# Order of loads, casts and second-layer splits around the first expert tile of an attention-plus-MoE kernel

## Chip, cores and metric

The kernel runs on one core of one Trainium2 chip. The metric is the device time of one execution in microseconds (us). A core has five engines with instruction streams of their own: PE (TensorE, matrix products), DVE (VectorE), ACT (ScalarE), POOL (GpSimd) and SP (SyncE, which here only issues transfers). Each works through its stream in order and waits on semaphores for the others. PEld is PE loading weights. Transfers issued by SP and by POOL stand in two queues, called q1 (SP) and q0 (POOL) in the profile, which are served by the same 16 DMA engines.

## The reference

Softmax attention with capped scores, then a top-1 mixture of experts (MoE) with a modality bias on the gate. Sizes: 8 batches of 448 tokens, 12 heads of 64; 3584 tokens of width 768, 8 experts, inner width 1024; all in float32.

```python
scores = cap * np.tanh(scale * np.matmul(q, k.transpose(0, 1, 3, 2)) / cap)
attn = np.exp(scores - np.max(scores, axis=-1, keepdims=True))
attn = attn / (np.sum(attn, axis=-1, keepdims=True) + 1e-09)
attn_out = np.matmul(attn, v)                      # -> x: [3584, 768]
...
logits = x @ w_gate + modality_bias[modality_id]
e_idx = np.argmax(logits, axis=1)                  # one expert per token
gate_w = probs[np.arange(N), e_idx]
for e in range(E):
    mask = e_idx == e
    h = np.maximum(x[mask] @ w1[e], 0.0)
    out[mask] = gate_w[mask, None] * (h @ w2[e])
```

## The kernel before

**Attention** (the first 332 us) runs over 24 units d, each two head pairs of one batch (three units to a batch), in 7 steps s of 64 keys. PE makes scores (`sc`), ACT applies tanh and exp (`pt`), PE multiplies by the values (`xT`), DVE sums the weights (`tot`). Finished tokens are written to a table `xd` in DRAM. `route` picks each token's expert and scatters the token's number and gate weight into a map `mapd` in DRAM, grouped by expert, with four indirect transfers on POOL for each batch.

**The MoE part** works on slots: 384 tokens of one expert, in three row tiles t of 128. `rows` loads the slot's part of the map (`mt`, 3 KB), `gather` fetches the tokens with three indirect transfers on POOL (`xg`), PE transposes them (`move`), ACT and DVE write them as a high and a low half (`take`, tile `x`). The weights are split the same way: `split_w` has ACT cast a raw chunk to its high half (`ah` for the first layer, `bh` for the second) and DVE subtract that from the raw chunk for the low half (`al`, `bl`). The first layer's weights `w1` have 6 chunks of 512 KB (index k), the second layer's `w2` 8 chunks of 384 KB (index f). Raw chunks go through a ring of four buffers (`raw`); a load waits until the chunk that held its buffer has been split. `ffn1` makes `h` (tile `ph` to `hh`, `hl`), `ffn2` makes the output rows (`py`; ACT scales them into `ot`, and an indirect transfer on POOL writes them out). Every product is three matmuls: high by high, high by low, low by high.

**The first slot overlaps the end of attention.** From the counts of the first seven batches `early_slot` picks an expert with a full slot. At unit 22, step 2, SP is given the load of `mt`, then POOL the three gathers; chunks 0 and 1 of `w1` are loaded by SP, chunks 2 to 5 by POOL (`load_w1` inside `attention`; the last two have buffers of their own, `spare`). The slot's `ffn1` carries hooks. Its first three column tiles are made together, chunk by chunk (per chunk k three tiles of three matmuls), and after single chunks, and after column tile f = 3, a piece of leftover attention work is put in: `last_sums`, `last_turn`, `last_route`, `last_rank`, then `slots`, the table of all other slots. In this slot `ffn2` is called with `wait=2`: for t = 0 both halves of the output are accumulated side by side in the two `py` banks (f outermost), and the transposes of the next slot's tokens come only after the first half of t = 1.

**What sets the order.** A scheduler places instructions by dependences and by the order of the code; what is given to `pin` (and all loads made by `load`) keeps the program's order on its engine. A register load may be tied behind an instruction (`register(..., after)`). The splits of the second layer's first four chunks come after `slots` (hook f = 3), the next four after `ffn1`, and `load_w1` of the next slot's expert before `ffn2`.

Of the kernel before, what the change touches and what calls it, by code (L numbers as in the profile page):

```python
# [49 lines left out]
B, H, S, D = 8, 12, 448, 64  # L50
C, CP = 4, 112
NP = H // 2
NT, DM, FF, E, NM = B * S, H * D, 1024, 8, 2
# [14 lines left out]
ENDS = ((2, 2, 1), (3, 2), (3, 2, 1))  # L68
MAXS = RB + E - 1
W2_EARLY = 4  # L70
LEAD = 3
CAP_FAST = 64.0
NU = NP // 2
# [6 lines left out]
class Program:  # L80
# [340 lines left out]
    def attention(self, firsts, rp, xp):  # L421
        tc, nc = self.tc, self.nc
        pe, pin, V = nc.tensor, self.pin, nc.vector
        with ExitStack() as st:
# [154 lines left out]
            for n in range(END):  # L579
                d, s = divmod(n, STEPS)  # L580
                if s == 0:
                    fetch(d + 1)
                    if d == 0:
                        self.fetch_bias()
                    if d == 2:
                        self.empty_map()
                scores(n)
                while n not in held and added <= n - BEHIND + (d == ND - 1):
                    add(added)
                    added += 1  # L590
                if (d, s) == (1, 3):
                    self.gate_bias()
                if (s == 6 or s == 1) and d != SOON + 2:
                    go_on()
                if s == 4 and d >= 2 and d != SOON + 2:
                    turn(d - 2)
                    go_on()
                    tokens(d - 2)
                    logits(d - 2)
                if (d, s) == (SOON + 3, 0):  # L600
                    sums(d - 2)
                if s == 5 and d and d != SOON + 2:
                    sums(d - 1)
                    if d >= 2 and d - 2 != SOON and (d - 2) % NU == NU - 1:
                        start_route((d - 2) // NU)
                for m in due[n]:
                    weigh(m)
                    if m % STEPS == STEPS - 1:
                        keep(m // STEPS)
                if (d, s) == (SOON + 1, 6):  # L610
                    turn(SOON)
                    logits(SOON)
                    start_route(SOON // NU, firm=True)
                    go_on()
                    go_on()
                if (d, s) == (SOON + 2, 1):
                    go_on()
                    meta = self.early_slot(self.cpool, self.ps_r)
                    self.first_e = self.expert(meta, 0)
                    load_w1((0, 1), self.first_e)  # L620
                if (d, s) == (SOON + 2, 2):
                    tokens(SOON, nc.sync, (self.ps_r, "small"), (ps_g, "glog"))
                    maps = self.rows(meta, 0, early=True)
                    self.gather(maps, known=NT - S)
                    load_w1((2, 3, 4, 5), self.register(nc.gpsimd, meta[0:1, 0:1], E - 1), nc.gpsimd)
                if (d, s) == (SOON + 2, 6):
                    split(0, V, V)
                if (d, s) == (SOON + 3, 5):
                    split(1, V, V)
# [30 lines left out]

            def last_sums():
                ready(3)
                sums(ND - 1, self.ps_y, "py")

            def last_turn():
                ready(5)
                turn(ND - 2)
                logits(ND - 2)

# [62 lines left out]
    def gather(self, mt, n=TW, known=NT):  # L732

        for t in range(n):
            got = self.nc.gpsimd.indirect_dma_start(
                self.xg.bitcast(F32)[:, t], None, self.xd[:known],
                bass.IndirectOffsetOnAxis(ap=mt.bitcast(I32)[:, t, 0:1], axis=0),
                bounds_check=known - 1, oob_is_err=False,
            )
            self.pin(got)  # L740

    def load_raw(self, e, src, k, width, dst=None, queue=None):
        raw = self.stg.tile([128, FF], F32, name="raw") if dst is None else dst
# [89 lines left out]
            finish(ph, f)  # L833
            hook("f", f)

    def ffn2(self, mt, n, between=(), wait=0):

        nc = self.nc
        between = list(between)
        for t in range(n):  # L840
# [19 lines left out]
            for half in range(2):  # L860
                if not both:
                    for f in range(FC):
                        products(half, f)
                cs = slice(half * HALF, (half + 1) * HALF)
                nc.scalar.mul(ot[:, cs], pys[half][:, :HALF], mt[:, t, 1:2])  # L865
                left = 2 * n - 1 - (2 * t + half)
                if 2 * t + half >= wait:
                    for _ in range(-(-len(between) // left) if left else 0):
                        between.pop(0)()
# [5 lines left out]
    def run_slot(self, cur, n, ahead=None, raws=(), hooks=None):  # L875
# [5 lines left out]
        moves = []  # L881
        if hooks:
            work = hooks[("f", 3)]
            hooks[("f", 3)] = lambda: (work(), self.load_w2(cur[0], raws, range(W2_EARLY)))
        elif n == TW:
            self.load_w2(cur[0], raws)
        nxt = ahead() if ahead and not hooks else None
# [3 lines left out]
            nxt = ahead()  # L891
        if n < TW:
            self.load_w2(cur[0], raws)
        if nxt:
            self.load_w1(nxt[0])
            moves = [lambda k=k: self.transpose(k, self.ps_t, "ptr", n=nxt[2]) for k in range(KC)]
        self.ffn2(cur[1], n, between=moves, wait=2 if raws else 0)
        return nxt

    def run_slots(self, cur, hooks):  # L900
# [240 lines left out]
```

## Time and profile before

| | us |
|---|---|
| times of three runs | 868.88, 873.9, 873.51 (median 873.51) |
| profiled execution, its own time | 873.96 |
| its span, first to last instruction | 872.4 |
| PE busy in the span | 842.1 (97%) |
| ACT busy | 533.0 (61%) |
| DVE busy | 514.4 (59%) |
| POOL busy | 134.5 (15%) |
| DMA, mean over the span | 157 GB/s |

Times inside the profile count from the span's start. A row of the timeline gives start, duration, engine, line of the kernel, operation and tiles, and in brackets how long the engine was idle just before and what ended that. Line 767 is the transpose of gathered tokens, 777 and 778 ACT's and DVE's part of `take`, 753 and 754 those of `split_w`, 799, 800 and 803 the first layer's products, 850 the second layer's, 865 the scaling of output rows, 735 the gather, 726 the load of `mt`, 275 the scatter into the map, 547 the write of tokens to `xd`, 92 a load.

### The profile page before, as it was taken

To read this page: it belongs to the slowest core of one execution; us is meant where nothing else is said; L and a number is where in the kernel's file an instruction comes from. 1 tells how busy PE (TensorE), PEld (TensorE's weight loads), DVE (VectorE), ACT (ScalarE), POOL (GpSimd) and SP (SyncE) were. 2 spreads that over 40 slices of the span, in tenths; PEclk is the share of its full clock that TensorE was granted. 3 is DMA by queue.
4 is the path that set the end of the run, shared out by engine and by line. 5 is a ranking of instruction groups with operands and counts; after the bars stand their busy time and mean duration, and the time that the engine had idled before them with its cause. 6 is when DMAs were issued, how large, how long until landed. Compare 5 with 4: busy or idle time off the path is not lost. (4 is left out here: it accounts for less than half of the span.)

```text
span 872.4 us, 15882 instructions
## 1 busy us (share of the span) xinstructions
PE 842.1 (97%) x6216; PEld 639.4 (73%) x6216; DVE 514.4 (59%) x896; ACT 533.0 (61%) x627; POOL 134.5 (15%) x155
## 2 busy tenths in 40 slices
PE   7999999999999998989999999999999999999996
PEld 2344434434444336979999999999999999989995
DVE  3679687788888796854433444334344433467851
ACT  6999989999999894354342444334344433446541
POOL 2002020202020232242030120202002030011000
PEclk9999999999999998989999999999999999999998
DMA  5354444554453674297355473535646353457640
GB/s 168 105 170 100 156 135 144 143 166 98 165 123 132 170 185 130 46 323 238 95 168 196 144 255 105 189 109 173 223 139 228 115 156 142 158 158 240 225 159 6
DMA packets 44284, 136.92 MB, mean 157 GB/s; under 512 B 8526, under 2 KB 9102, under 8 KB 44192
## 3 DMA queue, kind: packets, MB, share of 16 engines
q1 hardware_dynamic: 34432, 101.00, 36.5%
q0 software_dynamic: 9616, 34.74, 13.2%
q8 instruction: 52, 0.85, 0.4%
q14 instruction: 40, 0.33, 0.1%
q10 hardware_dynamic: 144, 0.00, 0.0%
HBM read 114.20 MB, written 22.69 MB: 157 GB/s over the span
## 5 line engine op out<-in xcount | busy, mean ns | idle before, releaser
L459 ACT ACTIVATE pt<-sc,isc 128x896 f32<-128x896 f32 x168 | 161.3, 995 | 17.2 <-PE sc L455 17.0
L803 PE MATMUL ph<-x,al 128*128 128x384 f32 (+2 forms) x528 | 167.9, 318 | 0.0
L850 PE MATMUL py<-bh,hh 128*128 128x384 f32 x464 | 160.2, 345 | 4.9 <-ACT ot L865 3.3
L850 PE MATMUL py<-bl,hh 128*128 128x384 f32 x464 | 157.1, 339 | 0.6 <-DVE bl L754 0.6
L850 PE MATMUL py<-bh,hl 128*128 128x384 f32 x464 | 157.1, 339 | 0.0
L462 ACT ACTIVATE pt<-pt,cabs 128x1792 f32<-128x1792 f32 x84 | 150.4, 1790 | 2.7
L485 PE MATMUL xT<-pt,va 64*64 64x448 f32 x1344 | 146.2, 538 | 0.3 <-DVE xT L492 0.3
L473 DVE TENSOR_TENSOR tot<-tot,pt 128x896 f32<-128x896 f32 x120 | 130.3, 1086 | 7.5 <-ACT pt L462 4.1
L800 PE MATMUL ph<-x,ah 128*128 128x384 f32 x384 | 129.2, 336 | 0.4 <-DVE x L778 0.4
L799 PE MATMUL ph<-x,ah 128*128 128x384 f32 x384 | 129.5, 337 | 0.0
L754 DVE TENSOR_TENSOR bl<-raw,bh 128x768 fp32r<-128x768 f32 x88 | 81.3, 955 | 50.5 <-ACT bh L753 44.0
L485 PEld LDWEIGHTS xT<-pt,va 64*64 64x64 f32 x1344 | 50.0, 133 | 79.2 <-issue 68.2
L753 ACT CAST bh<-raw 128x768 fp32r<-128x768 f32 x88 | 70.3, 840 | 55.7 <-DMA raw<-in_w_dram 51.0
L803 PEld LDWEIGHTS ph<-x,al 128*128 128x128 f32 x528 | 102.1, 193 | 0.0
L811 ACT ACTIVATE hh<-ph 128x384 fp32r<-128x384 f32 x64 | 30.7, 490 | 103.2 <-PE ph L803 93.2
L865 ACT ACTIVATE ot<-py,mt 128x384 f32<-128x384 f32 x58 | 33.6, 581 | 98.4 <-issue 49.6
L850 PEld LDWEIGHTS py<-bh,hh 128*128 128x128 f32 x464 | 88.0, 190 | 5.9 <-ACT ot L865 3.6
L870 POOL DMA_INDIRECT out_dram<-ot,mt x29 | 31.5, 1086 | 387.1 <-ACT ot L865 314.0
L754 DVE TENSOR_TENSOR al<-raw,ah 128x1024 fp32r<-128x1024 f32 x64 | 76.3, 1222 | 21.9 <-ACT ah L753 20.3
L850 PEld LDWEIGHTS py<-bl,hh 128*128 128x128 f32 x464 | 88.0, 190 | 0.8 <-DVE bl L754 0.8
L850 PEld LDWEIGHTS py<-bh,hl 128*128 128x128 f32 x464 | 88.0, 190 | 0.2 <-DVE hl L812 0.2
L778 DVE TENSOR_TENSOR x<-ptr,x 128x384 fp32r<-128x384 f32 (+2 forms) x64 | 31.8, 516 | 93.9 <-ACT x L777 93.7
(160 smaller groups left out, 1043.0 us busy)
## 6 DMA issues: line engine op xcount, KB each, us to landing
raw<-in_w_dram SPq DMA_DIRECT2D x88, 384.0 KB, 5.0
raw<-in_w_dram SPq DMA_DIRECT2D x62, 512.0 KB, 4.8
kq<-in_kq_dram SPq DMA_DIRECT2D x24, 448.0 KB, 6.1
va<-in_v_dram SPq DMA_DIRECT2D x24, 448.0 KB, 6.8
kx<-in_kq_dram SPq DMA_DIRECT2D x24, 448.0 KB, 5.1
xd<-xs POOLq DMA_DIRECT2D x23, 448.0 KB, 5.1
raw<-in_w_dram POOLq DMA_DIRECT2D x2, 512.0 KB
spare<-in_w_dram POOLq DMA_DIRECT2D x2, 512.0 KB
```

The costliest lines, as they stand in the source:

```text
L459: pin(nc.scalar.activation(weights(n), sc[:, :, :S], AF.Tanh, scale=self.isc))
L462: pin(nc.scalar.activation(pt, pt, AF.Exp, scale=self.cabs))
L473: pin(V.tensor_tensor(tots[d], pt_of(n - 1) if s == 1 else tots[d], pt_of(n), op=ALU.add))
L485: pin(pe.matmul(self.xT[j * D : (j + 1) * D, i, :S], vas[d][rows, o : o + D], pt[rows, j], start=s == 0, stop=s == STEPS - 1,))
L753: keep((cast.tensor_copy if cast else self.nc.scalar.copy)(hi, raw))
L754: keep((minus or self.nc.vector).tensor_tensor(lo, raw, hi, op=ALU.subtract))
L778: keep(nc.vector.tensor_tensor(lo, pt[:, :w], hi, op=ALU.subtract))
L799: keep(nc.tensor.matmul(ph[:, :w], hi[:, fs], self.x[:, k, 0, :w], start=first, stop=False))
L800: keep(nc.tensor.matmul(ph[:, :w], hi[:, fs], self.x[:, k, 1, :w], start=False, stop=False))
L803: keep(nc.tensor.matmul(ph[:, :w], lo[:, fs], self.x[:, k, 0, :w], start=False, stop=last))
L850: nc.tensor.matmul(pys[half][:, :HALF], self.h[a][:, f, rows], self.w2s[f][c][:, cs], start=f == i == 0, stop=f == FC - 1 and i == 2,)
L865: nc.scalar.mul(ot[:, cs], pys[half][:, :HALF], mt[:, t, 1:2])
```

## The change

Three edits, all around the first slot.

1. The register that the loads of chunks 2 to 5 need is read on POOL only behind the last of the three gathers; so the gathers come ahead of these loads in POOL's stream.
2. Of the second layer's chunks, 0 and 1 are split inside `ffn1` (in `last_sums` and `last_turn`) and no longer after `slots`; chunks 2 and 3 stay there.
3. In the first slot, `load_w1` of the next expert (loads and splits) is called by `ffn2` after both scalings of the first row tile, which are now pinned, and no longer ahead of `ffn2`.

```diff
+W2_FIRST = 2
@@ attention
-                    self.gather(maps, known=NT - S)
-                    load_w1((2, 3, 4, 5), self.register(nc.gpsimd, meta[0:1, 0:1], E - 1), nc.gpsimd)
+                    got = self.gather(maps, known=NT - S)
+                    load_w1((2, 3, 4, 5), self.register(nc.gpsimd, meta[0:1, 0:1], E - 1, got.ins), nc.gpsimd)
             def last_sums():
                 ready(3)
+                self.load_w2(None, self.raws, range(1))
                 sums(ND - 1, self.ps_y, "py")
             def last_turn():
                 ready(5)
+                self.load_w2(None, self.raws, range(1, W2_FIRST))
                 turn(ND - 2)
@@ gather
             self.pin(got)
+        return got
@@ ffn2
-    def ffn2(self, mt, n, between=(), wait=0):
+    def ffn2(self, mt, n, between=(), wait=0, then=None):
-                nc.scalar.mul(ot[:, cs], pys[half][:, :HALF], mt[:, t, 1:2])
+                put = nc.scalar.mul(ot[:, cs], pys[half][:, :HALF], mt[:, t, 1:2])
+                if both:
+                    self.pin(put)
+                    if half:
+                        then()
@@ run_slot
-            hooks[("f", 3)] = lambda: (work(), self.load_w2(cur[0], raws, range(W2_EARLY)))
+            hooks[("f", 3)] = lambda: (work(), self.load_w2(cur[0], raws, range(W2_FIRST, W2_EARLY)))
+        then = lambda: self.load_w1(nxt[0])
         if nxt:
-            self.load_w1(nxt[0])
+            if not hooks:
+                then()
-        self.ffn2(cur[1], n, between=moves, wait=2 if raws else 0)
+        self.ffn2(cur[1], n, between=moves, wait=2 if hooks else 0, then=then if hooks else None)
```

POOL, from the last scatters into the map before the first slot; before:

```order
L275 DMA mapd<-pay_3103,pos 31104x2 x4
L99 TENSOR_LOAD emeta
L99 ISA x2
L92 ISA
L92 DMA raw<-in_w_dram 128x1024
L92 ISA
L92 DMA raw<-in_w_dram 128x1024
L92 ISA
L92 DMA spare<-in_w_dram 128x1024
L92 ISA
L92 DMA spare<-in_w_dram 128x1024
L735 DMA xg<-xd,mt 128x768 x3
```

and of the change (all lines after the first edit are numbered one to eight higher there):

```order
L276 DMA mapd<-pay_3103,pos 31104x2 x4
L738 DMA xg<-xd,mt 128x768 x3
L102 TENSOR_LOAD emeta
L102 ISA x2
L93 ISA
L93 DMA raw<-in_w_dram 128x1024
L93 ISA
L93 DMA raw<-in_w_dram 128x1024
L93 ISA
L93 DMA spare<-in_w_dram 128x1024
L93 ISA
L93 DMA spare<-in_w_dram 128x1024
```

The four loads and the read of the expert's number have moved behind the three gathers; the next write of tokens (`xd`) still comes after both.

ACT, from the last first-layer columns of the first slot to the first tokens of the next slot (`bh` second-layer chunks of this slot, `ah` first-layer chunks of the next); before:

```order
L811 ACTIVATE hh<-ph 128x384 x4
L753 CAST bh_3802<-raw 128x768
L753 CAST bh_3804<-raw 128x768
L753 CAST bh_3806<-raw 128x768
L753 CAST bh_3808<-raw 128x768
L753 CAST ah_160<-raw 128x1024
L753 CAST ah_162<-raw 128x1024
L865 ACTIVATE ot<-py,mt 128x384 x2
L753 CAST ah_164<-raw 128x1024
L753 CAST ah_166<-raw 128x1024
L753 CAST ah_168<-raw 128x1024
L865 ACTIVATE ot<-py,mt 128x384
```

and of the change:

```order
L815 ACTIVATE hh<-ph 128x384 x4
L757 CAST bh_3806<-raw 128x768
L757 CAST bh_3808<-raw 128x768
L757 CAST bh_3810<-raw 128x768
L757 CAST bh_3812<-raw 128x768
L869 ACTIVATE ot<-py,mt 128x384 x2
L757 CAST ah_160<-raw 128x1024
L757 CAST ah_162<-raw 128x1024
L757 CAST ah_164<-raw 128x1024
L757 CAST ah_166<-raw 128x1024
L869 ACTIVATE ot<-py,mt 128x384
```

Two casts of the next expert's chunks stood ahead of the two scalings; now none does, and four stand between them and the third.

PE, where the last batch is routed during column tile f = 4 of `ffn1` (`rank` counts the tokens ahead of each token, `ph` is the first layer's product, `tp` transposes tokens); before:

```order
L799 MATMUL ph<-x,ah_160 128x384
L258 LDWEIGHTS tri
L258 MATMUL rank<-oh,tri 112x32
L800 MATMUL ph<-x,ah_160 128x384
L803 MATMUL ph<-x,al_161 128x384
L799 MATMUL ph<-x,ah_162 128x384
L260 LDWEIGHTS ones
L260 MATMUL rank<-before,ones 112x32
L538 MATMUL tp<-ident,xT 112x128 x8
```

and of the change:

```order
L803 MATMUL ph<-x,ah_160 128x384
L804 MATMUL ph<-x,ah_160 128x384
L259 LDWEIGHTS tri
L259 MATMUL rank<-oh,tri 112x32
L807 MATMUL ph<-x,al_161 128x384
L803 MATMUL ph<-x,ah_162 128x384
L804 MATMUL ph<-x,ah_162 128x384
L807 MATMUL ph<-x,al_163 128x384
L803 MATMUL ph<-x,ah_164 128x384
L804 MATMUL ph<-x,ah_164 128x384
L261 LDWEIGHTS ones
L261 MATMUL rank<-before,ones 112x32
```

The second `rank` product, on which the table of the other slots hangs, stands four first-layer matmuls later than before.

## Rows read from the trace of the kernel before

**Rows 1.** Stretches: length, busy us of PE, PEld, DVE, ACT, POOL, TensorE clock, DMA.

```profile
332.40:336.27 3.87, 0.37 (x2) 0.19 (x2) 0.19 (x1) 0.75 (x1) 0.65 (x1) 0.76 0.87 306
336.27:341.10 4.83, 4.83 (x25) 4.83 (x26) 3.91 (x6) 4.43 (x8) 0.00 (x0) 0.50 0.01 6
...
379.87:383.16 3.29, 0.00 (x1) 0.00 (x1) 1.73 (x2) 1.82 (x4) 3.00 (x5) 0.85 0.93 320
383.16:388.90 5.74, 5.74 (x18) 5.74 (x19) 3.17 (x3) 2.40 (x3) 2.53 (x4) 0.50 1.02 382
...
404.00:750.00 346.00, 346.00 (x2046) 344.72 (x2045) 147.88 (x191) 143.88 (x229) 43.56 (x39) 1.00 0.50 167
```

**Rows 2.** Waits of PE, 332 to 404 us: total, times, longest.

```profile
PE ptr L767 <- DMA xg<-xd,mt: 3.5, 2, 2.0
PE py L850 <- ACT ot L865: 3.3, 1, 3.3
PE py L850 <- DVE bl L754: 0.6, 1, 0.6
```

**Rows 3.** Timeline of POOL around the first gather.

```profile
310.95 1.17 POOL L92 DMA_DIRECT2D raw<-in_w_dram  x2
...
327.08 1.06 POOL L735 DMA_INDIRECT xg<-xd,mt  x1 [13.92 <-DMA mt<-mapd]
...
330.46 1.80 POOL L735 DMA_INDIRECT xg<-xd,mt  x1 [0.30 <-DVE tot L473]
```

**Rows 4.** Timeline of SP in the same stretch.

```profile
312.10 0.68 SPq L547 DMA_DIRECT2D xd<-xs  x1
319.64 0.35 SPq L726 DMA_DIRECT2D mt<-mapd  x1
```

**Rows 5.** DMA queues from 319 to 324 us: packets, MB, share of 16 engines.

```profile
q0 software_dynamic: 286, 1.03, 76.1%
q1 hardware_dynamic: 266, 0.27, 15.4%
```

**Rows 6.** Timeline of ACT after attention's last product.

```profile
332.25 0.91 ACT L492 COPY xT<-xT 128x896 f32<-128x896 f32 x1 [2.43 <-PE xT L485]
336.67 0.86 ACT L777 CAST x<-ptr 128x384 fp32r<-128x384 f32 x2 [3.52 <-PE ptr L767]
```

**Rows 7.** Timeline of DVE, first chunks of the first slot.

```profile
337.19 0.56 DVE L778 TENSOR_TENSOR x<-ptr,x 128x384 fp32r<-128x384 f32 x1 [4.60 <-ACT x L777]
...
345.55 0.62 DVE L503 COPY gl<-glog 128x448 f32<-128x448 f32 x1 [3.14 <-PE glog L501]
...
347.22 0.55 DVE L778 TENSOR_TENSOR x<-ptr,x 128x384 fp32r<-128x384 f32 x1
```

**Rows 8.** Costliest groups of the page: a second-layer split's part on DVE.

```profile
L754 DVE TENSOR_TENSOR bl<-raw,bh 128x768 fp32r<-128x768 f32 x88 | 81.3, 955 | 50.5 <-ACT bh L753 44.0
```

**Rows 9.** Timeline of ACT at the end of the first row tile.

```profile
381.58 1.04 ACT L753 CAST ah<-raw 128x1024 fp32r<-128x1024 f32 x1 [1.47 <-DMA raw<-in_w_dram]
382.53 1.05 ACT L865 ACTIVATE ot<-py,mt 128x384 f32<-128x384 f32 x2
```

**Rows 10.** Timeline of PE: the first transposes of the next slot's tokens.

```profile
390.11 0.62 PE L767 MATMUL ptr<-identr,xg 128*128 128x128 f32 x6
```

**Rows 11.** Timeline of POOL around the next slot's gather.

```profile
369.17 0.55 POOL L726 DMA_DIRECT2D mt<-mapd  x1 [1.16 <-issue]
...
377.16 1.29 POOL L735 DMA_INDIRECT xg<-xd,mt  x1 [4.69 <-issue]
...
380.10 1.00 POOL L735 DMA_INDIRECT xg<-xd,mt  x1 [0.30 <-PE py L850]
...
387.21 0.76 POOL L724 DMA_DIRECT2D mt<-mapd  x1 [1.17 <-DMA xg<-xd,mt]
```

**Rows 12.** Tile xg, 395 to 460 us: from issue to landing.

```profile
DMA to landing us min/median/max: 6.0/6.0/6.0
```

**Rows 13.** Tile mt, 300 to 400 us: from issue to landing.

```profile
DMA to landing us min/median/max: 3.1/5.9/8.2
```

## The prediction

> **What bounds the kernel now.** I read the waits of PE first, then stretches around each wait with the granted clock, then the timelines of the engine that ended each wait. From 404 to 750 us PE is busy in every microsecond, 2046 matmuls in 346 us, 0.169 us each [rows 1]: there nothing but PE counts, and time won ahead of it is won for the whole kernel unless the end eats it. The change touches the stretch from attention's end (332.4 us) to 404 us. PE waits there in two places, and both cost twice, once as idle time and once as clock.
>
> First place: attention's last product ends at 332.4, the first gather is not there, PE stands until 336.27 with one short transpose in between, 3.5 us of waiting [rows 1, 2]. After it the clock is granted at 0.50, the lower of the two levels (1.2 GHz), for 4.83 us [rows 1].
>
> Second place: the first row tile of the first slot's second layer ends at 379.87. The two `py` banks it filled must be scaled out by ACT before PE goes on, and ACT is in line behind two casts of the next expert's chunks, which wait for their loads; the scaling starts at 382.53 [rows 9]. PE waits 3.3 us [rows 2], then runs at 0.50 for 5.74 us, 18 matmuls of 0.319 us [rows 1].
>
> **Part 1, first gather and loads.** POOL starts four loads (2 MB) at 310.95 and the first gather at 327.08, 13.9 us idle for `mt` [rows 3]. SP issued `mt` at 319.64, so it was 7.4 us on the way, behind the write of `xd` in the same queue [rows 4]. Meanwhile POOL's queue moved 1.03 MB and SP's 0.27 MB [rows 5]. With POOL's loads gone from there, `mt` should land sooner. Bounds: 3.1 us is the fastest landing of an `mt` in this stretch [rows 13], giving a first gather at 322.7; the other bound is 327.08, as now. The third gather started 3.4 us after the first [rows 3] and needs 6.0 us to land [rows 12], so all tokens are there between 332.1 and 336.5. I take the early end, since what sat on the engines is what is removed; then PE's wait is gone.
>
> What is late next is the chain of halves: ACT's copy of the last `xT` ends at 333.16 [rows 6], and only then can it cast the first tokens, 3.5 us sooner than the 336.67 of now. From there to the end of chunk 4's `x` on DVE (347.77) [rows 7] the chain took 11.1 us, 3.14 of it DVE idle while PE, at the low clock, had not made `glog`. In that gap now stands the split of second-layer chunk 0, 0.96 us [rows 8]. So chunk 4 is ready at 333.16 + 11.1 - 3.14 + 0.96 = 342.1 instead of 347.8: **5.7 us won**. That holds both the idle time and the clock of the first place; the most would be 3.9 + half of 4.83 = 6.3, the least 0.
>
> The loads of chunks 2 to 5 pay for it: they start when the third gather is issued, about 5.2 us after the first [rows 3], so at 327.9. 2.1 MB take 5.5 us at the 382 GB/s of the second place [rows 1] or 10.2 us at the 0.21 MB/us that POOL's queue had beside others [rows 5]; the last chunk is there by 333.4 to 338.1 plus a latency, put at 3.1 us [rows 13]. Chunk 2 is to be cast at 334.0, chunk 5 at about 341. A quarter of the loads takes 1.4 to 2.6 us, so both are met. Cost nothing; the cover is the time of the chain above.
>
> **Part 2, splits of second-layer chunks 0 and 1.** Their 0.96 us on DVE each and as many casts on ACT move to where DVE idles (chunk 0) and behind chunk 5 (chunk 1), where DVE is on the way to the next table but soon waits for ACT again: nothing. What they give: the ring buffers of chunks 4 and 5 come free early, and 6 and 7 have only two splits ahead of them. PE's wait of 0.6 us for `bl` goes [rows 2]: **0.6 us won**. If it stays, that is lost.
>
> **Part 3, the next expert's casts behind the scalings.** Nothing stands ahead of the scalings but casts that PE itself needs. The first half's last product lies three matmuls (0.5 us) ahead of the tile's end, and PE went on 0.63 us after ACT began (383.16 against 382.53) [rows 1, 9], so 0.2 us of wait remain: **3.1 us won**, and with no idle time no clock is lost: 18 x (0.319 - 0.169) = **2.7 us**. The casts start a little later than now and would have to be over 10 us late to be missed by the next slot's first layer.
>
> **What takes part of it back.** PE transposes the next slot's tokens after half of the second row tile, at 390.11 now, without waiting [rows 10]. Their gather was not early: `mt` issued at 369.17, gathers at 377.16 to 380.10, and at 387.21 POOL was still released by one of them [rows 11]. In the clock of before (all of it moved by part 1's 5.7 us alike): the first row tile now ends at 379.87 - 0.6, and half a tile later, 24 x 0.169 = 4.1 us and the 0.2 of wait, PE wants the tokens at 383.6. The table the gather hangs on needs the `rank` product, which now stands four matmuls later, 4 x 0.169 = 0.7 us. So the third gather starts at 380.8 and lands 6.0 us later [rows 12] at 386.8: PE **waits 3.2 us**. Bounds: with an `mt` landing in 3.1 instead of the 8.0 us between 369.17 and 377.16, no wait at all; with the gather taking the whole time to 390.1, as far as the rows exclude more, 7.2 us. I take 6.0, because the loads that shared the engines with it will be partly done. Both waits of this length, 3.9 and 3.3 us, were followed by the low clock [rows 1], so I charge that again: **2.7 us**. The scalings' stall moves to the transposes.
>
> **The sum.** 5.7 + 0.6 + 3.1 + 2.7 - 3.2 - 2.7 = 6.2 us. The profiled execution took 873.96 us (its span 872.4), 0.45 over the median of 873.51. **873.96 - 6.2 = 867.8 us**. Own range of this case 865.5 to 870.5.
>
> **Rivals.** (a) *The second gather is in time or nearly so, and the clock holds.* For it: the loads of chunks 4 and 5 are out of the way by then, and `mt` (3 KB) has landed in 3.1 us elsewhere in the stretch [rows 13]. Then neither 3.2 nor 2.7 is charged: 861.9; with 2 us of wait at the full clock 863.9. A page points this way: the Trainium skill, DMA: Bandwidth & Descriptors, section on the anatomy of one DMA on the gpsimd path, gives such a transfer a fixed cost of about 2 us plus its bytes at 436 GB/s. By that rule `mt` would land at 371.9 in the clock of before and the wait be gone, so 861.9. The trace disagrees: 8.0 us until the gather that needs it started [rows 11], though some of that was not the transfer's.
> (b) *The first gather isn't sooner.* `mt` waits for the scatters into the map and then for the `xd` write, and neither needs POOL's loads gone. For it: SP sent `mt` only at 319.64, 8.7 us after POOL began the loads [rows 3, 4]. Part 1 gives nothing: 873.96 - (0.6 + 3.1 + 2.7 - 3.2 - 2.7) = 873.5.
> (c) *Slower: the loads are late.* If in (b) the third gather still ends at 332.3 [rows 3], chunks 2 to 5 start at about 333, and chunk 2 is due for its cast at 338, chunk 5 at 346.7 (a cast of 1.04 [rows 9] before DVE's turn after 347.77). At 0.21 MB/us and 3 us of latency as above they land at 338.6 and 346.2, so this decides at that rate; any slower and PE waits microsecond by microsecond. 3 us late and the clock lost once more give 873.5 + 5.7 = 879.2.
>
> **How the numbers follow.** Forecast 0.46; (a) 0.34; (b) 0.13; (c) 0.05; the rest lies between. The range of 8 in 10 takes in (a) with almost no wait and the worst gather (7.2 us of wait, 4 more than charged: 871.8): 862.0 to 872.0. One per cent, about what a measurement here can tell from no change, is 8.7 us, so faster by more means under 864.8: most of (a), 0.30. Slower by more, over 882.2, is the far part of (c), 0.03. Within: 0.67.
>
> **What would show it.** Right: PE goes from attention into the transposes at 332 us with no wait and a clock of 1.00; the first gather starts on POOL at 320 to 323; no load of raw chunks ends an ACT wait before 345; ACT's two scalings start within 0.2 us of PE's last products; and PE's longest wait between 332 and 404 is for `xg`, at about 378 us, some 3 us long, followed by 0.50. Wrong: a gather still at 327 (b); ACT waiting for raw chunks 2 to 5 (c); transposes without a wait (a); or a low clock in the first layer though nothing waited.

## The result, and the profile after

The changed kernel takes 861.89 us (median of four runs, 860.25 to 863.89) against 871.34 for the kernel before beside it: ratio 0.9892, 95% interval 0.9846 to 0.9938. A later comparison gave 0.9893 (0.9872 to 0.9915). So it is 1.1% faster, 9.4 us, where 6.2 us were forecast; the time lies 5.9 us under the forecast and just under the low end of the range. The profiled execution took 860.5 us, its span is 858.9.

Waits of PE from 320 to 404 us in the changed kernel, answering to [rows 2] (total, times, longest):

```profile
PE ptr L771 <- DMA xg<-xd,mt: 1.6, 2, 0.9
PE ph L804 <- DVE x L782: 0.4, 1, 0.4
PE ph L803 <- DVE x L782: 0.4, 1, 0.4
```

The waits for the scalings (3.3 us) and for `bl` (0.6) are gone, and the 3.5 us for the first gather too: the 1.6 us named here for `xg` is another one, the next slot's. The timeline of PE shows it, answering to [rows 10] (start, duration, then in brackets the idle time ahead and what ended it):

```profile
332.22 0.70 PE L771 MATMUL ptr<-identr,xg 128*128 128x128 f32 x6
...
377.52 0.22 PE L771 MATMUL ptr<-identr,xg 128*128 128x128 f32 x1
378.64 0.28 PE L771 MATMUL ptr<-identr,xg 128*128 128x128 f32 x1 [0.90 <-DMA xg<-xd,mt]
379.64 0.53 PE L771 MATMUL ptr<-identr,xg 128*128 128x128 f32 x4 [0.72 <-DMA xg<-xd,mt]
```

At 332.22 PE goes from attention into the transposes without a gap. At 377.52 it finds one of three groups of the next slot's tokens and waits for the other two. Stretches of the changed kernel, answering to [rows 1] (start:end, length, busy us of PE, PEld, DVE, ACT, POOL, then the granted TensorE clock, DMA share, GB/s):

```profile
334.30:339.00 4.70, 4.70 (x27) 4.62 (x27) 4.70 (x7) 4.08 (x6) 0.00 (x0) 1.00 1.01 345
...
380.20:383.60 3.40, 3.40 (x12) 3.40 (x12) 2.25 (x3) 2.65 (x4) 1.46 (x2) 0.50 1.03 356
383.60:387.00 3.40, 3.40 (x24) 3.37 (x23) 1.23 (x1) 1.03 (x4) 0.11 (x1) 0.99 0.82 239
...
395.00:741.00 346.00, 346.00 (x2047) 344.96 (x2046) 146.78 (x190) 142.93 (x228) 42.85 (x38) 1.00 0.50 167
```

The first layer runs at 1.00 where it ran at 0.50. Behind the new wait the clock is at 0.50 for 3.4 us and then back, half as long as behind either wait of before. There it fell while PE was still waiting, so the stretches of [rows 1] show only the part of it in which PE worked. For the second wait (kernel before):

```profile
382.20:389.00 6.80, 5.84 (x18) 5.84 (x19) 3.68 (x3) 3.36 (x5) 3.42 (x6) 0.50 1.03 379
```

The long stretch of the changed kernel is the same as before, 2047 matmuls for 2046.

POOL around the first gather, answering to [rows 3], and SP, answering to [rows 4]:

```profile
323.87 1.22 POOL L738 DMA_INDIRECT xg<-xd,mt  x1 [12.81 <-DMA mt<-mapd]
...
326.72 1.51 POOL L738 DMA_INDIRECT xg<-xd,mt  x1 [0.30 <-issue]
328.23 1.18 POOL L93 DMA_DIRECT2D raw<-in_w_dram  x2
```

```profile
312.21 0.68 SPq L548 DMA_DIRECT2D xd<-xs  x1
321.41 0.35 SPq L729 DMA_DIRECT2D mt<-mapd  x1
```

`mt` was issued later than before (321.41 for 319.64) and the gather still started sooner: 2.5 us from the one to the other for 7.4. ACT at both places, answering to [rows 6, 9]:

```profile
333.16 0.87 ACT L781 CAST x<-ptr 128x384 fp32r<-128x384 f32 x2
...
335.62 1.05 ACT L757 CAST ah<-raw 128x1024 fp32r<-128x1024 f32 x1 [0.27 <-DMA raw<-in_w_dram]
...
338.13 1.05 ACT L757 CAST ah<-spare 128x1024 fp32r<-128x1024 f32 x1 [0.35 <-DMA spare<-in_w_dram]
...
372.61 1.10 ACT L869 ACTIVATE ot<-py,mt 128x384 f32<-128x384 f32 x2 [2.37 <-PE py L854]
```

The first tokens are cast at 333.16, as soon as the copy allows. Chunks 3 and 4 of the weights were waited for, 0.27 and 0.35 us: the loads are later and only just in time. The scalings begin 0.14 us ahead of PE's last product of the tile (its start is 372.75) and end a wait for PE, no longer one for loads.

How the gain builds up, by the start of the same instruction in the timelines of PE:

| place on PE | before | after | won so far | by the forecast |
|---|---|---|---|---|
| chunk 4's second product, first layer | 347.83 | 342.48 | 5.35 | 5.7 |
| last product of row tile 0 | 379.53 | 372.75 | 6.78 | 6.3 |
| row tile 1 begins | 383.16 | 373.24 | 9.92 | 9.4 |
| first transposes of the next tokens | 390.11 | 377.52 | 12.59 | 12.1 |
| first product behind them | 390.57 | 380.01 | 10.56 | 8.9 |
| second transposes | 394.82 | 385.83 | 8.99 | 6.2 |
| slot 1's first layer | 404.30 | 395.31 | 8.99 | 6.2 |
| end of the span | 872.4 | 858.9 | 13.5 | 6.2 |

Two differences remain to be explained: the new wait and its clock took back 3.6 us and not 5.9, and the two profiled executions differ by 4.5 us more behind slot 1, where nothing was changed. The last slots show what the latter is. Before, then after, around the end of the last slot's first layer:

```profile
846.40:853.30 6.90, 6.90 (x33) 6.90 (x34) 4.13 (x14) 1.48 (x5) 0.00 (x0) 0.51 0.01 2
```

```profile
836.90:843.80 6.90, 6.87 (x55) 6.75 (x54) 4.30 (x17) 1.67 (x6) 0.00 (x0) 1.00 0.01 2
```

The profiled execution of before fell to 0.50 there and made 33 matmuls in the time of 55. At half the clock 6.9 us cost some 3.4 us of the 4.5.

### The profile page after: what moved, and what is told of

It is laid out like the page before. It is cut to its first block, busy times and chain, and to the rows that moved or that the text cites. A ratio compares the mean times of both kernels' runs of the same rounds, so it can differ in the third digit from the quotient of the medians.

```text
span 858.9 us, 15884 instructions
## 1 busy us (share of the span) xinstructions
PE 834.9 (97%) x6216; PEld 632.2 (74%) x6216; DVE 514.0 (60%) x896; ACT 532.7 (62%) x627; POOL 133.5 (16%) x155
## 5 line engine op out<-in xcount | busy, mean ns | idle before, releaser
L807 PE MATMUL ph<-x,al 128*128 128x384 f32 (+2 forms) x528 | 165.9, 314 | 0.0
L807 PEld LDWEIGHTS ph<-x,al 128*128 128x128 f32 x528 | 99.3, 188 | 0.0
```

The lines of the kernel that those rows point to most:

```text
L807: keep(nc.tensor.matmul(ph[:, :w], lo[:, fs], self.x[:, k, 0, :w], start=False, stop=last))
```

## The experiments

One measure serves for all: from the first transposes of the first slot (`ptr`, 332.11 us in the kernel before) to slot 1's first product, the "start" below, from the timeline of PE of one execution. It leaves out attention and the last slots. The ratios are to the kernel before on the same chip; its medians on the three chips were 869.7, 867.2 and 870.6 us, so times of different comparisons are set side by side by ratio.

| kernel | median us | ratio (95%) | start us | PE waits for the next gather, for the scalings, us |
|---|---|---|---|---|
| before | 871.34 | 1 | 72.2 | 0, 3.3 |
| before, again | 870.96 | 0.9998 (0.998 to 1.0017) | 72.3 | 0, 2.9 |
| edit 1 | 865.78 | 0.9953 (0.9934 to 0.9973) | 66.4 | 0, 3.8 |
| edit 2 | 867.33 | 0.9973 (0.9955 to 0.9991) | 68.6 | 1.9, 0.9 |
| edit 3 | 868.06 | 0.9979 (0.9963 to 0.9994) | 70.6 | 2.4, 0 |
| edits 1, 2 | 860.32 | 0.991 (0.9889 to 0.993) | 65.3 | 0, 3.3 |
| edits 1, 3 | 863.43 | 0.9941 (0.9918 to 0.9964) | 67.3 | 3.1, 0 |
| edits 2, 3 | 864.6 | 0.9974 (0.9955 to 0.9992) | 66.0 | 1.2, 0 |
| all three (the change) | 861.89 | 0.9892 (0.9846 to 0.9938) | 63.1 | 1.6, 0 |
| all three, again | 859.16 | 0.9893 (0.9872 to 0.9915) | 64.7 | 3.0, 0 |
| the change, half the loads ahead | 861.12 | 0.9873 (0.985 to 0.9896) | 63.2 | 1.7, 0 |
| the change, later transposes | 858.16 | 0.9874 (0.9847 to 0.99) | 59.8 | 0, 0 |
| the same, again | 859.52 | 0.9859 (0.9834 to 0.9883) | 59.9 | 0, 0 |
| edits 1, 2, later transposes | 860.72 | 0.988 (0.9853 to 0.9908) | 62.0 | 0.3, 2.0 |

Where the first and the next gather are waited for in one kernel, the gaps in PE's timeline tell them apart.

**Edit 1 alone**

```diff
+                    got = self.gather(maps, known=NT - S)
-                    load_w1((2, 3, 4, 5), self.register(nc.gpsimd, meta[0:1, 0:1], E - 1), nc.gpsimd)
+                    load_w1((2, 3, 4, 5), self.register(nc.gpsimd, meta[0:1, 0:1], E - 1, got.ins), nc.gpsimd)
@@ gather
+        return got
```

> Edit 1 alone (the first gather ahead of the loads of chunks 2 to 5 on POOL; casts and splits as before). Theory A, the terms read off the two traces (coupled parts): chunk 4's second product starts at 342.5 us instead of 347.8, which is 5.3 us; the 3.1 us behind row tile 0's last product, the clock of 0.50 after it and the 0.6 us for bl stay, each 5.3 us earlier; the next slot's gather also comes some 5 us earlier, so that PE (transposes at about 384.8) does not wait for it. Slot 1's first layer starts at about 399.0 us (before 404.3, after 395.3), and the time is 871.3 - 5.3 = 866.0 us. Rival B, the gain of the change is all in edit 1 (the idle time behind row tile 0 would close by itself when the tile is earlier): slot 1's first layer at 395 to 396 us, about 862 us.

Measured: 3.9 us faster by the medians, start 66.4, first gather at 321.63, chunk 4's second product at 341.82. The part of the gain ahead of row tile 0 is theory A's. The wait for the scalings stayed, and it showed something unexpected. Stretches of edit 1 alone, the wait and what follows:

```profile
374.20:378.00 3.80, 0.04 (x1) 0.05 (x1) 1.33 (x2) 1.62 (x3) 2.81 (x6) 1.00 0.94 383
```

```profile
378.60:382.00 3.40, 3.40 (x12) 3.40 (x12) 1.31 (x2) 1.91 (x2) 1.16 (x2) 0.50 1.04 341
382.00:385.40 3.40, 3.40 (x24) 3.37 (x23) 2.44 (x3) 2.48 (x5) 0.67 (x1) 0.99 1.02 366
```

PE stood 3.8 us, longer than the 3.3 us of before [rows 1], and the clock was low for only 3.4 us; in the kernel before the stretch from 382.30 to 389.00 us reads 0.50 throughout. So the price of the clock behind a wait isn't fixed by the length of the wait. B fell: the scalings' wait does not close by itself.

**Edit 2 alone**

```diff
+W2_FIRST = 2
@@ last_sums, last_turn
+                self.load_w2(None, self.raws, range(1))
+                self.load_w2(None, self.raws, range(1, W2_FIRST))
@@ run_slot
-            hooks[("f", 3)] = lambda: (work(), self.load_w2(cur[0], raws, range(W2_EARLY)))
+            hooks[("f", 3)] = lambda: (work(), self.load_w2(cur[0], raws, range(W2_FIRST, W2_EARLY)))
```

> Edit 2 alone (second-layer chunks 0 and 1 split during the first layer's row tile). Theory A: the two splits lie on ACT and DVE in time in which both wait for chunk 4's load, the bl wait of 0.6 us goes and with it up to 0.8 us of small waits at the end of the first layer: 0.6 to 1.4 us, 870 to 870.7 us, which the comparison cannot tell from none; the profile's list of PE waits has no wait for bl. Rival B: the splits stand ahead of chunk 4's cast and delay it: second product of chunk 4 at 349 us or later (before 347.8), 872.5 us or more.

Measured: 2.4 us faster. That is more than either theory gave, though A's 0.6 to 1.4 lies inside the interval (0.8 to 3.9 us). Waits of PE, 320 to 415 us:

```profile
PE ptr L770 <- DMA xg<-xd,mt: 5.0, 3, 1.9
PE py L853 <- ACT ot L868: 0.9, 1, 0.9
```

The `bl` wait is gone, as A says, and chunk 4 is not delayed (347.05), against B. What A did not have: the wait for the scalings shrank from 3.3 to 0.9 us with the casts still ahead of them, and 1.9 of the 5.0 us for `xg` is already the next gather's. Of the 3.6 us in the start, 0.9 were won ahead of chunk 4's second product, where the first wait was 0.5 us shorter and the low clock behind it 3.4 us long for 6.8; edit 2 changes nothing about that wait.

**Edit 3 alone**

```diff
...
-                nc.scalar.mul(ot[:, cs], pys[half][:, :HALF], mt[:, t, 1:2])
+                put = nc.scalar.mul(ot[:, cs], pys[half][:, :HALF], mt[:, t, 1:2])
+                if both:
+                    self.pin(put)
+                    if half:
+                        then()
...
```

`then` is `load_w1` of the next expert, which `run_slot` hands over instead of calling it ahead of `ffn2`.

> Edit 3 alone (next expert's casts behind row tile 0's two scalings). Theory A (the parts are coupled through the next slot's gather): the idle time of 3.1 us behind row tile 0 goes, PE comes to the transposes at about 384.3 us, but the gather's third part lands only at 388.8 us as in the kernel before, so that PE waits about 4.5 us there and the granted clock falls again: transposes end at 389.3 (before 390.6), and the low clock after it takes the rest: 870 to 872.7 us, no gain that can be measured. Rival B (the parts add up, as the sum on record has it for the idle time and the clock): 3.1 + 2.7 us, 865.5 us.

Measured: 1.6 us faster. The scalings' wait went, and PE waited 2.4 us for the next gather instead, the clock falling behind it. Rival B, 5.8 us, is out. A has the place right and the size too large (4.5 us of wait): the gather's third part started 1.7 us sooner than in the profile of before (378.40 for 380.10). A's total, no gain that can be measured, is out as well.

**The change with the transposes half a row tile later**

```diff
-                left = 2 * n - 1 - (2 * t + half)
-                if 2 * t + half >= wait:
+                left = 2 * n - (2 * t + half) - (0 if wait else 1)
+                if 2 * t + half >= (wait and 3):
```

> The changed kernel with the transposes of the next slot's tokens half a row tile later (2 behind each of the last three halves instead of the middle three). Theory A: the 2.0 us that PE waits for the next gather and the 1.6 us of low clock after it are all that the coupling still costs: the first transposes come at about 381.7 us, after the gather's last part has landed at 379.6, there is no wait for xg and no clock of 0.50 from 380 to 384; slot 1's first layer at about 391.7 us (after 395.3) and 861.9 - 3.6 = 858.3 us. Rival B: the last two chunks' transposes and casts, now behind the last product of the slot, are late for slot 1's first products, which gives 1 us or more back, or the clock falls elsewhere: 860 to 862 us.

Measured: 858.16, start 59.8 against 63.1, which is 3.3 us of the 3.6. The timeline of PE has the next tokens' transposes without any wait, and the stretch around them the full clock:

```profile
381.29 0.63 PE L771 MATMUL ptr<-identr,xg 128*128 128x128 f32 x6
...
386.00 0.91 PE L771 MATMUL ptr<-identr,xg 128*128 128x128 f32 x6
```

```profile
377.00:382.00 5.00, 5.00 (x34) 4.96 (x33) 1.86 (x2) 0.76 (x3) 3.14 (x5) 1.00 0.92 282
382.00:387.00 5.00, 4.98 (x32) 4.69 (x31) 3.38 (x4) 3.98 (x7) 0.75 (x1) 1.00 0.91 298
```

So what the changed kernel still loses between 332 and 404 us is the wait for the next gather and the low clock behind it. In the totals the step from the change (0.9892, 0.9893) to this version (0.9874, 0.9859) is 1.6 to 3 us, no more than the intervals allow for sure; in the start it is 3.3 to 4.9.

**The change without edit 3, without edit 2, without edit 1**

Each is the changed kernel with one of the three diffs above taken back.

> The changed kernel without edit 3 (edits 1 and 2; casts of the next expert ahead of the scalings again). Theory C, from edit 2 alone: the early splits free staging buffers sooner, so that the next expert's loads and casts end sooner, and the scalings wait only about 0.9 us behind row tile 0 instead of 3.3; what is left of edit 3 is taken out of PE's wait for the next gather (2.0 us in the changed kernel). From PE's first transpose of the first slot to its first product of slot 1: 63 to 64 us (changed kernel 63.1), total within 1 us of the changed kernel. Rival D, the sum on record (edit 3 alone closes the 3.1 us and saves the clock behind them): 2 to 6 us slower than the changed kernel.

Measured: 1.2 us over the changed kernel of the same comparison, within the intervals; start 65.3 against 64.7. D's 2 to 6 us did not come, though the intervals don't exclude its low end. C was right for a wrong reason: the early splits did not shorten the scalings' wait, it was back in full (from the waits of PE):

```profile
PE py L854 <- ACT ot L869: 3.3, 1, 3.3
```

What the kernel loses there it doesn't lose at the transposes, which now come after the gather (no wait for `xg`). The length of this wait, 0.9 to 3.8 us in the kernels without edit 3, goes with the load that the last cast ahead of the scalings needs: ACT waited 2.38 us for it here and 0.21 with edit 2 alone.

> The changed kernel without edit 2 (edits 1 and 3; no second-layer split during the first layer's row tile). Theory C: the small waits for bl of about 1.0 us come back in row tile 0, but PE then waits that much less for the next gather, which lands at the same time: from the first transpose to slot 1's first product 63 to 63.6 us, total as the changed kernel. Rival D (the parts add up): 0.6 to 1.4 us slower.

Measured: 4.3 us over the changed kernel of the same comparison, and the intervals don't touch. Both theories were too low. In its profile row tile 0 ends 1.5 us later by the waits for `bl` and smaller ones; then PE still waits 3.1 us for the next gather, and the clock is low for the whole stretch behind it:

```profile
377.90:384.80 6.90, 6.04 (x21) 5.86 (x22) 4.70 (x5) 4.25 (x6) 1.82 (x2) 0.51 0.93 317
```

By the mean granted clock of its runs (0.9927, the changed kernel 0.9950) about 2 of the 4.3 us are clock. That profile is the slowest of its executions (866.67 us), so the rest isn't accounted for beyond those 1.5 us.

> The changed kernel without edit 1 (edits 2 and 3, first gather again behind the loads of chunks 2 to 5). Theory C: edit 1 sets when the next slot's gather lands; without it the gather's last part lands at about 385 us, as with edit 2 alone, so that edits 2 and 3 together bring no more than the better of them alone: from the first transpose to slot 1's first product 68 to 70 us (edit 2 alone 68.6, edit 3 alone 70.6, before 72.2), 866.5 to 868 us. Rival D, the terms on record add up (0.6 for bl, 3.1 idle, 2.7 clock): 863.5 to 865 us.

Measured: ratio 0.9974, as edit 2 alone (0.9973) and edit 3 alone (0.9979). D, 0.991 to 0.993 by its times, is out. By the medians the two others bring no more together without edit 1 than each alone; the two gains added up would make 0.9952, which the intervals don't exclude. The next gather's third part starts at 374.73, 46.5 us behind the first transposes, while it is at 41.1 to 42.7 in every kernel with edit 1. PE gets to the transposes at 50.3 and waits 1.2 us, the longer part here:

```profile
380.19 0.53 PE L770 MATMUL ptr<-identr,xg 128*128 128x128 f32 x4 [0.72 <-DMA xg<-xd,mt]
```

The start of 66.0 is under the expected 68 to 70. This profile is the fastest of 12 executions, without a low clock behind the wait; its mean granted clock is 0.995, that of the twelve 0.9919, so its start makes the kernel look better than it mostly is.

**The change again, and the kernel before again**

No edit in either.

> The changed kernel itself, beside the others of this call, and a second profile of it. All theories: 860 to 864 us. If the end of the slots' loop falls to 0.50 in one execution and not in another, its profiles differ by 3 to 4 us in the stretch from slot 1 on; if the length of a stretch of low clock belongs to the stall before it, the stretch behind the transposes of slot 1's tokens is again 3.4 us long.

> The kernel before itself, for a second profile and its spread beside the kernels of this call. Theory E: the profiled execution from which the sum was made (873.96 us, clock 0.985) stood at the slow end; what differs between executions is the length of the low clock behind a wait (3.4 or 6.8 us, 1.7 us of time for each 3.4) and whether the last slots fall too. So this profile has the same waits (first gather about 3.5 us in all, scalings about 3.3, bl about 0.6), fewer microseconds at 0.50 ahead of slot 1 or none near 846 us, and a median of 867 to 870 us. Rival F: the lengths belong to the waits: 6.8 us behind both waits again and a fall near 846 us, 873 us.

Measured for the change: start 64.7, since PE waited 3.0 us for the same gather that cost 1.6 in the first profile; the low clock was again 3.4 us long. Measured for the kernel before: start 72.3, within 0.1 us of the first profile, waits 3.9, 2.9 and 0.9, and then, at the last slot:

```profile
382.30:388.10 5.80, 5.56 (x17) 5.56 (x18) 3.42 (x3) 2.92 (x5) 3.50 (x6) 0.50 1.04 377
...
846.40:853.20 6.80, 6.70 (x51) 6.73 (x52) 4.05 (x16) 1.86 (x6) 0.00 (x0) 1.00 0.01 2
```

So E and F share this: the long low clock behind the first two waits came again (F), the fall near 846 us did not (E), the median of 870.96 lies between theirs, and the span is 868.0, 4.4 us less than that of the profile from which the sum was made. From slot 1 to the end it takes 464.3 us here and 468.1 there; over all fourteen profiles 463.6 to 469.3, with no order by edits. Of 75 executions of the kernel before in these comparisons, 4 took 873.9 us or more.

**The change with half of the loads ahead of the gather**

```diff
+                    load_w1((2, 3), self.register(nc.gpsimd, meta[0:1, 0:1], E - 1), nc.gpsimd)
                     got = self.gather(maps, known=NT - S)
-                    load_w1((2, 3, 4, 5), self.register(nc.gpsimd, meta[0:1, 0:1], E - 1, got.ins), nc.gpsimd)
+                    load_w1((4, 5), self.register(nc.gpsimd, meta[0:1, 0:1], E - 1, got.ins), nc.gpsimd)
```

> The changed kernel, but the loads of chunks 2 and 3 ahead of the first gather again and 4 and 5 behind it. Theory G: what made the first gather late are the loads' bytes that share the DMA engines with the small read of the map and the gather's rows: with half of them ahead (1.05 MB instead of 2.1) the wait for the first gather lies between: 1 to 2.5 us of PE's wait for xg from 328 to 338 us (all four ahead: 3.0 to 3.5; none: 0), and the transfer of the map's rows takes 4 to 6 us (7.4 with all, 2.5 with none). Total 1 to 3 us over the changed kernel. Rival H: the order on POOL's queue alone decides, however little is ahead: a wait of 3 us or more, as with all four.

Measured: no wait for the first gather, 0.9873, the same as the change. POOL and SP, then the DMA queue from 319 to 324 us:

```profile
311.02 1.18 POOL L93 DMA_DIRECT2D raw<-in_w_dram  x2
323.90 1.16 POOL L739 DMA_INDIRECT xg<-xd,mt  x1 [11.70 <-DMA mt<-mapd]
```

```profile
319.79 0.35 SPq L730 DMA_DIRECT2D mt<-mapd  x1
```

```profile
q0 software_dynamic: 33, 0.11, 6.0%
```

H fell: two loads ahead do no harm. G's transfer time came (4.1 us from `mt` to the gather, between 2.5 and 7.4), its wait did not. The queue row fits that: POOL's queue moved only 0.11 MB at that time, against 1.03 MB in the kernel before [rows 5]. So what is ahead of `mt` seems to count by what is left of it when `mt` is issued. That is argued from these kernels and not tested further: edit 1 alone, with no load ahead, took 3.4 us, not far from the 4.1.

**Later transposes without edit 3, and with it again**

The diff of the later transposes above, once with the diff of edit 3 taken back and once as it is.

> The version with the transposes half a row tile later, without edit 3. Theory C: edit 3 brought little in the changed kernel (about 1 us between the two medians) because PE then waited for the next slot's gather instead; where the transposes come after the gather, nothing takes the time back, and the 3.3 us wait for the scalings and the low clock behind it (1.7 to 3.4 us) count in full: 4.5 to 7 us slower than the same version with edit 3, that is 862.5 to 865 us on a chip on which that one takes 858. Rival D: edit 3 is worth about 1 us there too: 859 us.

> The changed kernel with the transposes of slot 1's tokens half a row tile later, again, beside the others of this call: no wait for xg between 370 and 395 us, no clock of 0.50 between 372 and 395 us, from the first transpose of the first slot to slot 1's first product about 59.8 us (changed kernel 63.1 and 63.8), ratio to the kernel before 0.985 to 0.990.

Measured: 860.72 without edit 3, 859.52 with it; starts 62.0 and 59.9. Theory C's 4.5 to 7 us fell. The wait for the scalings was only 1.4 us behind row tile 0 here (0.6 of the 2.0 in the table came later) and no low clock followed it, so the start is 2.1 us worse and no more:

```profile
376.00:382.00 6.00, 6.00 (x37) 6.00 (x36) 1.66 (x2) 0.71 (x1) 3.93 (x7) 1.00 0.93 337
```

The later transposes themselves did again what was expected: no wait for `xg`, start 59.9, against 63.1 and 64.7 (not 63.8, as the expectation has it) in the changed kernel. This version, with all three edits, has the lowest ratio in both comparisons that hold it, within the intervals.

## Why the prediction was right or wrong

**Part 1 (5.7 us) was right, with half of its reason.** The first gather is no longer waited for, and chunk 4's `x` ended on DVE at 342.42 (341.87 + 0.55) for 342.1. The gather was to start at 320 to 323 and started at 323.87; it was in time all the same. Rival (b)'s doubt held for one half: SP's issue of `mt` did not come sooner. In all fourteen profiles it lies 8.6 to 11.3 us behind POOL's last scatter, with the loads there or not. The other half, the transfer of `mt`, is what the loads made long: 6.8 to 7.7 us to the first gather in the five profiles with all four loads ahead, 2.5 to 4.1 in the nine others. The delayed loads were hidden, with almost nothing to spare (0.27 and 0.35 us of waiting on ACT).

**Part 2 (0.6 us) was too small.** Row tile 0 ended 6.78 us earlier with chunk 4 only 5.35 us earlier, so some 1.4 us were won between: the other small waits of the second layer and the table (0.3 for `bh`, 0.3 for the rank) went with the one for `bl`, which makes 1.1 us by the rows. Taking edit 2 back cost 1.5 us there, and 4.3 us in the median.

**Part 3 (3.1 and 2.7 us) was right in its size and not in its worth.** Row tile 1 began 3.14 us sooner against the tile's end, and the clock held. But as a part of the sum it isn't edit 3's: taken back alone, edit 3 costs 1.2 us, since PE without it comes to the transposes when the gather is there. The "taken back" step belonged to it, as the sum had it.

**"What takes part of it back" was the step that failed in the sum:** the right place, time and mechanism, at 378 us as foreseen, and 5.9 us charged for 3.6. The wait cost 2.03 us for 3.2. The third gather was to start at 380.8 in the clock of before, 375.1 with part 1's 5.7 us taken off, and started at 373.80, since 6.7 us lay between `mt` and the first gather and not 8.0. In the second profile of the change these are 7.9 us, and PE waited 3.0 us; so this term lies inside what executions differ by. The clock cost 1.6 for 2.7: the sum took the 5.7 us at 0.50 of [rows 1] for the price of a wait, and that was one of two lengths seen. Behind waits of 1.6 to 3.9 us the low clock lasted 3.4 us in seven profiles (both of the change, half the loads, each edit alone, edits 2 and 3) and 6.8 in both of the kernel before and in two others (edits 1, 2 and edits 1, 3); the waits of 3.8 and 3.9 us had the short one. At half speed the short one costs 1.7 us, the long one 2.4 to 3.0, as PE works in 4.9 to 6.0 us of it. Sum with the measured terms: 5.35 + 1.43 + 3.14 + 2.67 - 2.03 - 1.57 = 8.99 us, against 6.2.

**The base was the other error.** The sum was set against 873.96 us. Some 3.4 of it are the fall at 846 us, in a stretch no edit touches, and the second profile of the kernel before does not have it. Two of the three times shown agreed with it by chance; over 75 executions 873.9 is the slow end. Of the 5.9 us, 2.6 are the base (873.96 against 871.34) and the other 3.25 the effect (9.45 against 6.2).

**The rivals.** (a) named the measured time, 861.9, and not what happened: the wait is there in both profiles of the change and the clock fell. That the number agrees is luck. The range began at 862.0 and so left out (a)'s own time, though (a) had a chance of 0.34. What (a) needed was a short way from the next slot's `mt` to its gather, and its support for that, an `mt` landing of 3.1 us in [rows 13], was misread: those rows take in every transfer that writes or reads `mt`, and the 3.1 us are a write of output rows. The one landing of an `mt` among them took 8.2 us. Kernel before, `out_dram` from 385 to 400 us, then `mt` from 380 to 385:

```profile
DMA to landing us min/median/max: 3.1/3.1/3.1
```

```profile
DMA to landing us min/median/max: 8.2/8.2/8.2
```

The 3.1 us also stand in part 1, as the early bound of the first gather and as the latency of the loads. SP's `mt` landed 1.6 us after its issue in the two profiles with edit 1 that recorded it (the change again, later transposes); for the loads no row shows the 3.1. POOL, answering to [rows 11]:

```profile
363.87 0.54 POOL L729 DMA_DIRECT2D mt<-mapd  x1 [1.04 <-issue]
...
370.58 1.59 POOL L738 DMA_INDIRECT xg<-xd,mt  x1 [3.40 <-issue]
...
373.80 1.00 POOL L738 DMA_INDIRECT xg<-xd,mt  x1 [0.30 <-issue]
```

From the issue to the gather that needs it are 6.7 us, and 6.1 to 8.1 in all fourteen profiles (8.0 before). POOL issues two further loads of `mt` in that time, the last until 367.18, and then stands for 3.4 us. The transfer alone: five loads of this group whose landing is recorded, in four other profiles, took 4.4 to 5.9 us. The rule named for (a) was the fixed cost of about 2 us in the Trainium skill, DMA: Bandwidth & Descriptors, section on the anatomy of one DMA on the gpsimd path. The 4.4 to 5.9 us are two to three times that.

(b) is out by edit 1 alone. The sign named for (c), ACT waiting for raw chunks, did show, but with 0.6 us in all, and PE's wait for chunk 4's `x` stayed at 0.4 us.

What stays open: why the low clock is 3.4 us long behind one wait and 6.8 behind another of the same length; why PE found the clock at full speed behind waits of 1.2 us (edits 2, 3) and 1.4 us (later transposes without edit 3); and why taking back edit 2 costs 4.3 us where its profile shows 1.5 us and a longer low clock.

## What to carry to other kernels

When stalls stand one behind another on the same engine, price the next one first: with edit 2 or edit 3 alone the next slot's gather took up part of what came too early (waits of 1.9 and 2.4 us that the kernel before doesn't have), and the edit that also moved that gather, edit 1, is by the medians the one that costs most to take back (5.4 us). In the totals this interplay is not shown: the gains of the edits alone, 3.9, 2.4 and 1.6 us, add up to 7.9, and all three together gave 8.0 to 9.4, with intervals of 1.3 to 4 us either way. What a wait downstream costs can be tested by moving its consumer: half a row tile later, the wait for the gather and the low clock behind it were gone (3.3 and 4.9 us in the start). And take a second profile of the kernel before as the base, or compare only up to a marker behind the change: one execution's low clock in an untouched stretch cost more than most terms of the sum.

## What the runs showed of the hardware

The scatters into the map end late, and traffic explains only part of it. In the changed kernel the write of `xd` keeps the DMA engines busy up to about 316 us, but they are idle from 318.7 to 321.4, when SP, which waits for the map, issues `mt` (DMA by fortieths of 310 to 322 us, tenths and GB/s):

```profile
DMA  0009410799999999999495271344100000000000
GB/s 0 0 0 191 27 27 27 246 369 382 437 410 396 412 341 348 362 369 137 48 58 24 21 17 24 31 38 75 44 17 7 0 0 0 0 0 0 0 0 0
```

POOL issued the last of them at 310.11, so the chain from there to SP took 11.3 us, and 8.6 with edit 3 alone, whose four loads moved at that time. The second of the four scatters landed 8.9 to 11.0 us after its issue in the ten profiles that recorded it (9.9 in the kernel before), scatters of the next batch, at about 350 us, 3.2 to 4.1 us after theirs. Why the former are so late is open.

The low clock's two lengths are the other thing: 3.4 us at 0.50 after 3.8 us of standing, 6.8 after 2.9 (the kernel before, again). Part of the spread between executions of one kernel goes with it: in four sets of executions of the kernel before, the times correlate at 0.58 to 0.94 with the time lost to the clock, estimated as (1 - clock) x span. The mean granted clock over a run was 0.985 to 0.996 in the 75 executions of the kernel before, and its average was 0.9904 for the kernel before against 0.9950 for the changed one (second comparison). The same estimate gives 8.3 us lost for the first and 4.3 for the second: half of the 8 us by which their means differ.
